# A two-layer block with Mish: the opening's loads of x and w1 cut and ordered anew

## The chip, the cores and the metric

The kernel runs on one core of one Trainium2 chip. The metric is the time of one execution on the device in microseconds, the median of several runs; lower is better. Before the change it is 105.08 us, the median of three runs from 104.75 to 105.43 us.

A core has TensorE (matrix products, from SBUF into the eight banks of PSUM), VectorE, ScalarE (activation functions), GpSimd and SyncE. In the profile they are PE (with PEld for its weight loads), DVE, ACT, POOL and SP. Loads and stores between DRAM and SBUF are DMAs. In this kernel SyncE and ScalarE issue them, each into a queue of its own, called a ring here: q1 is SyncE's and q10 ScalarE's in the profile.

## The reference

```python
B, S, D, F = 1, 2048, 512, 1792          # all bf16
h   = einsum("bsd,df->bsf", x, w1) + b1
sp  = log1p(exp(-abs(h))) + where(h > 0, h, 0)   # softplus
act = h * tanh(sp)                               # Mish
out = einsum("bsf,fd->bsd", act, w2)
```

Both products have the same number of multiplications: 2048 x 512 x 1792.

## The kernel before, in words

All sizes are cut into 128s: x has 16 tiles of 128 rows, D has 4 parts (index k), F has 14 (index f). The work goes through four blocks of 512 rows of x, that is four x tiles each (`BLOCKS`).

*First matmul* (`mm1_step`, L157, its product at L169). For each f, four products over k add up in one PSUM bank. The stationary operand is a 128x128 piece of w1, the moving one the transposed x: 128 rows (D) by up to 512 columns (rows of x). ScalarE then applies Mish with the bias (`mish`, L149) and writes the bf16 result into `a_sb`; this frees the bank.

*Second matmul* (`mm2_step`, L186). For each x tile, 14 products over f add up in a bank; `put` (L194) has VectorE copy the bank to `o_sb` and SyncE store it.

After the first block the order is regular: 14 f tiles of the first matmul, then the block's four x tiles of the second. The order of instructions on each engine is written out by hand; a wait on a semaphore stops its engine's stream, and all that comes later on that engine waits too. `wait` (L17) leaves out waits that the engine has already made.

*The opening* is where the change lies. While the first data travel, TensorE runs dummy products on a constant into bank 7 (`WARM`, L7). x is needed transposed. The first two tiles are loaded as they are into `x_nat` by one DMA on SyncE's ring (L102), a partition holding two neighbouring rows of x (2 KB in DRAM); TensorE transposes them in eight steps (`transpose_x`, L142) into banks 0 to 3, and VectorE and ScalarE in turn copy each k to `xT` (L145). The output rows of these two tiles are interleaved in the same way (`rows`, L180). All other x tiles come by DMA transpose straight into `xT`: tiles 2 and 3 at once (L103), each later block in one (L114).

w1 for the first eight f tiles comes in four DMAs, each of two k by four f tiles, with rows of 1 KB in DRAM: f 0 to 3 on ScalarE's ring, f 4 to 7 on SyncE's behind the x loads. Then SyncE loads the bias b1, the rest of w1 (768 KB), w2 (1792 KB) and the later x blocks.

In the first block, f 0 to 3 are computed on x tiles 0 and 1 (256 columns, all k), then on tiles 2 and 3 (`first`, L209). f 4 to 6 follow at 512 columns in two halves of k (`half`, L216), with the transpose of the bias (L234) between them, which reads the padded copy that VectorE makes (L230). The other f tiles follow at 512 columns.

Of the kernel before, what the change touches and what calls it, by code (L numbers as in the profile page):

```python
# [4 lines left out]

P = 128
WARM = (512,) * 5 + (256, 256)  # L7
BLOCKS = (512, 512, 512, 512)


# [21 lines left out]
def bass_standalone__dense_activation_mish__prompt_kernel(  # L32
# [20 lines left out]
    F0 = 4  # L53
    N0 = BLOCKS[0] // P

    with ExitStack() as es:
# [19 lines left out]
        sp = Stream(nc.sync, None)  # L76
# [5 lines left out]
        def load(q, dst, src, name, transpose=False):  # L82
            s = sem(name)
            (q.eng.dma_start_transpose if transpose else q.eng.dma_start)(dst, src).then_inc(s, 16)
            return (s, 16)
# [3 lines left out]

        t_w1, t_w2 = {}, {}
# [37 lines left out]

        free = [[] for _ in range(8)]
        t_cp = {(j, k): t_x23 for j in (2, 3) for k in range(KT)}
        t_mish, t_acc = {}, {}

        def transpose_x():

            pe.wait(t_xn, t_id)
            for k in range(KT):
                eng = (dve, act)[k % 2]
                psb = ps[:, k, 0:P].bitcast(BF)  # L140
                for j in range(2):
                    mm = nc.tensor.transpose(psb[:, j * P:(j + 1) * P], x_nat[:, j, k * P:(k + 1) * P], ident[:, :])  # L142
                eng.wait(pe.mark(mm))
                dst = xT[:, k, 0:2 * P]
                t = eng.mark(nc.vector.tensor_copy(dst, psb) if eng is dve else act.eng.activation(dst, psb, ACT.Copy))  # L145
                t_cp[0, k] = t_cp[1, k] = t
                free[k] = [t]

        def mish(s, f, bank, t_mm):  # L149
            n = BLOCKS[s]  # L150
            act.wait(t_b1c, t_mm)
            t = act.mark(act.eng.activation(a_sb[:, f, starts[s]:starts[s + 1]], ps[:, bank, 0:n], ACT.Mish,  # L152
                                            bias=b1_sb[:, f:f + 1]))
            t_mish[s, f] = t
            free[bank] = [t]

        def mm1_step(s, f, k, bank, js=None):  # L157

            n = BLOCKS[s]
            lo, hi = (0, n) if js is None else (js[0] * P, (js[-1] + 1) * P)  # L160
            first = k == 0 and lo == 0
            if first:
                pe.wait(*free[bank])
            pe.wait(t_w1[k, f])
            if s:
                pe.wait(t_xT[s])
            else:
                pe.wait(*[t_cp[j, k] for j in (js or range(N0))])
            return nc.tensor.matmul(ps[:, bank, lo:hi], w1_sb[:, k, f * P:(f + 1) * P],  # L169
                                    xT[:, k, starts[s] + lo:starts[s] + hi], start=first, stop=(k == KT - 1 and hi == n))  # L170
# [6 lines left out]
        s_out = sem("s_out")  # L177
        n_out = 0

        def rows(i):  # L180

            if i < 2:
                return out2[0:2 * P, :].rearrange("(p j) d -> p j d", p=P)[:, i, :]
            return out2[i * P:(i + 1) * P, :]
# [9 lines left out]
        def put(i, lo, hi, bank, t_mm):  # L194
            nonlocal n_out
            dve.wait(t_mm)
            t = dve.mark(nc.vector.tensor_copy(o_sb[:, i, lo:hi], ps[:, bank, 0:hi - lo]))  # L197
            free[bank] = [t]
            sp.wait(t)
            sp.eng.dma_start(rows(i)[:, lo:hi], o_sb[:, i, lo:hi]).then_inc(s_out, 16)  # L200
# [8 lines left out]
        def first(js, ks):  # L209
            for k in ks:  # L210
                for f in range(F0):
                    mm = mm1_step(0, f, k, 4 + f, js)
                    if k == KT - 1 and js[-1] == N0 - 1:
                        t_acc[f] = pe.mark(mm)

        def half(fs, ks):  # L216
            for f in fs:
                for k in ks:
                    mm = mm1_step(0, f, k, f - F0)
                if ks[-1] == KT - 1:  # L220
                    t_acc[f] = pe.mark(mm)
# [11 lines left out]
        psb1 = ps[:, 3, 0:P // 2].bitcast(BF)  # L233
        t_b1t = pe.mark(nc.tensor.transpose(psb1, b1_pad[:, :], ident[:, :]))  # L234
        dve.wait(t_b1t)
        t_b1c = dve.mark(nc.vector.tensor_copy(b1_sb[:, :], psb1[:, 0:FT]))  # L236
        free[3] = [t_b1c]
        for f in range(F0):
            mish(0, f, 4 + f, t_acc[f])
        half(range(F0, F0 + 3), (2, 3))  # L240
        for f in range(F0, F0 + 3):
            mish(0, f, f - F0, t_acc[f])
        for f in range(F0 + 3, FT):
            mm1(0, f, (4 + f) % 8)

        for i in range(N0):
            mm2(i, 0, D, (i + 2) % 4)
        for s in range(1, len(BLOCKS)):
            for f in range(FT):
                mm1(s, f, 4 + f % 4)  # L250
# [35 lines left out]
```

## Time and profile before

| what | value |
|---|---|
| median of three runs | 105.08 us |
| the profiled execution | 105.38 us |
| its span, first to last instruction | 104.1 us |
| TensorE busy | 100.8 us (97%) |
| ScalarE busy | 39.1 us (38%) |
| VectorE busy | 12.3 us (12%) |
| read from and written to DRAM | 3.94 and 2.10 MB |

The profile shows one execution. Times are in microseconds from the start of the span. A page of it gives each engine's busy time, the span in 40 slices, the DMA queues, the chain of work that ended last, and groups of instructions by line. Further views give the chain in order of time, the timeline of an engine, the waits, sums over stretches of time, and how long after its issue a DMA landed. Matmuls are pipelined, so that a group's busy time is not the sum of the durations of its instructions; the distance between starts is what one costs.

### The profile page before, as it was taken

To read this page: it belongs to the slowest core of one execution; us is meant where nothing else is said; L and a number is where in the kernel's file an instruction comes from. 1 tells how busy PE (TensorE), PEld (TensorE's weight loads), DVE (VectorE), ACT (ScalarE), POOL (GpSimd) and SP (SyncE) were. 2 spreads that over 40 slices of the span, in tenths; PEclk is the share of its full clock that TensorE was granted. 3 is DMA by queue.
4 is the path that set the end of the run, shared out by engine and by line. 5 is a ranking of instruction groups with operands and counts; after the bars stand their busy time and mean duration, and the time that the engine had idled before them with its cause. 6 is when DMAs were issued, how large, how long until landed. Compare 5 with 4: busy or idle time off the path is not lost.

```text
span 104.1 us, 1118 instructions
## 1 busy us (share of the span) xinstructions
PE 100.8 (97%) x485; PEld 48.2 (46%) x494; DVE 12.3 (12%) x22; ACT 39.1 (38%) x59; POOL 0.7 (1%) x6
## 2 busy tenths in 40 slices
PE   6999999999999999999999999999999999999992
PEld 2586444444444444444444444444444444444462
DVE  0200000022220000022220000022112000011223
ACT  3400999200027777200007777500005777700000
POOL 2000000000000000000000000000000000000000
PEclk9999999999999999999999999999999999999999
DMA  2999999991101000010111000001111000001111
GB/s 42 331 337 362 347 320 131 211 193 50 43 7 50 0 0 0 6 50 2 49 50 50 0 0 3 0 6 50 50 50 50 0 0 0 0 0 50 57 50 50
DMA packets 13345, 7.94 MB, mean 76 GB/s; under 512 B 7836, under 2 KB 13212, under 8 KB 13340
## 3 DMA queue, kind: packets, MB, share of 16 engines
q1 hardware_dynamic: 12796, 7.35, 27.0%
q10 hardware_dynamic: 544, 0.52, 1.4%
q8 instruction: 4, 0.07, 0.3%
q14 instruction: 1, 0.01, 0.0%
HBM read 3.94 MB, written 2.10 MB: 58 GB/s over the span
## 4 chain that ended last, share of the span: by engine, by line
PE 94%; DMA 3%; issue 1%; DVE 0%
PE ps L169 47%; PE ps L191 46%; DMA x_nat<-in_x_dram 3%; PE ps L142 1%; DVE o_sb L197 0%; PE ps L234 0%
## 5 line engine op out<-in xcount | busy, mean ns | idle before, releaser
L152 ACT ACTIVATE a_sb<-ps,b_sb 128x512 bf16<-128x512 f32 x56 | 37.1, 697 | 48.6 <-PE ps L169 43.3
L169 PE MATMUL ps<-xT,w_sb 128*128 128x512 bf16 (+1 forms) x235 | 49.3, 368 | 0.2
L191 PE MATMUL ps<-w_sb,a_sb 128*128 128x512 bf16 (+2 forms) x234 | 48.8, 366 | 0.3
L169 PEld LDWEIGHTS ps<-xT,w_sb 128*128 128x128 bf16 x240 | 23.7, 99 | 24.9
L191 PEld LDWEIGHTS ps<-w_sb,a_sb 128*128 128x128 bf16 x238 | 22.8, 98 | 25.9
L197 DVE CAST o_sb<-ps 128x512 bf16<-128x512 f32 (+2 forms) x17 | 11.2, 660 | 80.9 <-PE ps L191 80.9
L128 PE MATMUL ps<-const-bfloat16-1.0 128*128 128x512 bf16 (+1 forms) x7 | 2.7, 564 | 0.8 <-PEq L271 0.8
L122 ACT ACT_TABLE_LOAD x1 | 1.3, 1283 | 1.8 <-issue 1.8
L128 PEld LDWEIGHTS ps<-const-bfloat16-1.0 128*128 128x128 bf16 x7 | 0.9, 134 | 2.2 <-issue 2.2
L145 ACT ACTIVATE xT<-ps 128x256 bf16<-128x256 bf16 x2 | 0.8, 384 | 1.4 <-PE ps L142 1.3
L142 PE MATMUL ps<-ident,x_nat 128*128 128x128 bf16 x8 | 1.0, 311 | 0.2 <-DMA x_nat<-in_x_dram 0.2
L142 PEld LDWEIGHTS ps<-ident,x_nat 128*128 128x128 bf16 x8 | 0.8, 140 | 0.7 <-DMA x_nat<-in_x_dram 0.7
L145 DVE COPY xT<-ps 128x256 bf16<-128x256 bf16 x2 | 0.6, 292 | 3.3 <-PE ps L142 3.2
L230 DVE COPY b_pad<-b_nat 14x128 bf16<-14x128 bf16 x1 | 0.2, 183 | 3.1 <-DMA b_nat<-in_b_dram 3.1
L236 DVE CAST b_sb<-ps 128x14 f32<-128x14 bf16 x1 | 0.2, 173 | 2.2 <-PE ps L234 2.2
L120 POOL TENSOR_SCALAR_AFFINE_SELECT ident<-ones 128x128 bf16<-128x128 bf16 x1 | 0.3, 295 | 0.1
L234 PE MATMUL ps<-ident,b_pad 128*128 128x128 bf16 x1 | 0.2, 219 | 0.0
L117 DVE MEMSET b_pad<- 128x64 uint32 x1 | 0.1, 112 | 0.9 <-PEq L271 0.9
L118 POOL MEMSET ones<- 128x128 bf16 x1 | 0.2, 205 | 0.3 <-POOLq L271 0.3
L234 PEld LDWEIGHTS ps<-ident,b_pad 128*128 128x128 bf16 x1 | 0.1, 98 | 0.1
L271 POOL MEMSET const-bfloat16-1.0<- 128x1 bf16 x1 | 0.1, 102 | 0.0
L271 POOL MEMSET const-uint8-127<- 128x1 uint8 x1 | 0.1, 102 | 0.0
(2 smaller groups left out, 0.2 us busy)
## 6 DMA issues: line engine op xcount, KB each, us to landing
out_dram<-o_sb SPq DMA_DIRECT2D x15, 128.0 KB, 1.7
w_sb<-in_w_dram SPq DMA_DIRECT2D x1, 1792.0 KB, 10.4
w_sb<-in_w_dram SPq DMA_DIRECT2D x1, 768.0 KB, 5.6
w_sb<-in_w_dram ACTq DMA_DIRECT2D x2, 256.0 KB, 3.8
w_sb<-in_w_dram SPq DMA_DIRECT2D x2, 256.0 KB, 4.4
x_nat<-in_x_dram SPq DMA_DIRECT2D x1, 256.0 KB, 2.9
out_dram<-o_sb SPq DMA_DIRECT2D x1, 96.0 KB, 1.6
xT<-in_x_dram SPq DMA_TRANSPOSE x4, 5.5
```

The costliest lines, as they stand in the source:

```text
L118: t_ones = pool.mark(pool.eng.memset(ones[:, :], 1.0))
L120: t_id = pool.mark(pool.eng.affine_select(ident[:, :], ones[:, :], pattern=[[1, P]], compare_op=ALU.is_equal, fill=0.0, base=0, channel_mu ...
L122: act.eng.preload_act_table(ACT.Mish)
L128: nc.tensor.matmul(ps[:, 7, 0:n], c_w, c_m[:, 0:n], start=True, stop=True)
L142: mm = nc.tensor.transpose(psb[:, j * P:(j + 1) * P], x_nat[:, j, k * P:(k + 1) * P], ident[:, :])
L145: t = eng.mark(nc.vector.tensor_copy(dst, psb) if eng is dve else act.eng.activation(dst, psb, ACT.Copy))
L152: t = act.mark(act.eng.activation(a_sb[:, f, starts[s]:starts[s + 1]], ps[:, bank, 0:n], ACT.Mish, bias=b1_sb[:, f:f + 1]))
L169: return nc.tensor.matmul(ps[:, bank, lo:hi], w1_sb[:, k, f * P:(f + 1) * P], xT[:, k, starts[s] + lo:starts[s] + hi], start=first, stop=( ...
L191: return nc.tensor.matmul(ps[:, bank, 0:hi - lo], a_sb[:, f, i * P:(i + 1) * P], w2_sb[:, f, lo:hi], start=(f == 0), stop=(f == FT - 1))
L197: t = dve.mark(nc.vector.tensor_copy(o_sb[:, i, lo:hi], ps[:, bank, 0:hi - lo]))
L230: t_b1p = dve.mark(nc.vector.tensor_copy(b1_pad[0:FT, :], b1_nat[:, :]))
L234: t_b1t = pe.mark(nc.tensor.transpose(psb1, b1_pad[:, :], ident[:, :]))
```

## The change

- One dummy product of 256 columns is taken out.
- x tiles 0 and 1 are loaded by two DMAs of 128 KB, tile 0 on SyncE's ring, tile 1 on ScalarE's, each tile being 128 consecutive rows of x (1 KB rows). The interleaving and `rows` go.
- b1 is loaded second on ScalarE's ring.
- w1 for the first eight f tiles (`OPEN`) comes in four DMAs, each of one k and eight f tiles, with rows of 2 KB: k 0, 2 and 3 on SyncE's ring, k 1 on ScalarE's.
- The DMA transpose of x tiles 2 and 3 is issued after these.
- `transpose_x` takes one x tile at a time: two k to a bank and to a copy, VectorE k 0 and 1, ScalarE k 2 and 3.
- The first block runs k by k over eight f tiles in all eight banks (`bank0`): k 0 on tile 0 alone, then on tile 1 alone (128 columns each, f 0 to 6, as bank 7 is kept for the bias), the transpose of the bias, k 1 on both tiles, f 7 for k 0 and 1, then k 2 and 3; then tiles 2 and 3 for each f over all k, with its Mish behind it. f 8 to 13 follow at 512 columns.

```diff
-WARM = (512,) * 5 + (256, 256)
+WARM = (512,) * 5 + (256,)
...
-        for k0, k1 in ((0, 2), (2, 4)):
-            load_part(act, k0, k1, 0, F0)
-        t_xn = load(sp, x_nat[:, :, :], x2[0:2 * P, :].rearrange("(p j) d -> p j d", p=P), "s_xn")
+        for q, j in ((sp, 0), (act, 1)):
+            t_xn[j] = load(q, x_nat[:, j, :], x2[j * P:(j + 1) * P, :], "s_xn%d" % j)
+        t_b1 = load(act, b1_nat[:, :], b1.rearrange("(j p) -> j p", p=P), "s_b1")
+        for q, k in ((sp, 0), (act, 1), (sp, 2), (sp, 3)):
+            load_part(q, k, k + 1, 0, OPEN)
         t_x23 = load(sp, xT[:, :, 2 * P:4 * P], x2[2 * P:4 * P, :], "s_x23", True)
-        for k0, k1 in ((0, 2), (2, 4)):
-            load_part(sp, k0, k1, F0, 8)
-        t_b1 = load(sp, b1_nat[:, :], b1.rearrange("(j p) -> j p", p=P), "s_b1")
-        load_part(sp, 0, KT, 8, FT)
+        load_part(sp, 0, KT, OPEN, FT)
...
+        def transpose_x(j):
+            pe.wait(t_xn[j], t_id)
+            for h, eng in enumerate((dve, act)):
+                psb = ps[:, 2 * j + h, 0:P].bitcast(BF)
+                for i in range(2):
+                    k = 2 * h + i
+                    mm = nc.tensor.transpose(psb[:, i * P:(i + 1) * P], x_nat[:, j, k * P:(k + 1) * P], ident[:, :])
+                eng.wait(pe.mark(mm))
+                dst = xT[:, 2 * h:2 * h + 2, j * P:(j + 1) * P]
...
+        bank0 = (4, 5, 6, 0, 1, 2, 3, 7, 4, 5, 6, 0, 1, 2)
+
+        def first(fs, js, ks):
             for f in fs:
                 for k in ks:
-                    mm = mm1_step(0, f, k, f - F0)
...
+                    mm = mm1_step(0, f, k, bank0[f], js)
+            return mm
+
+        most, last = range(OPEN - 1), (OPEN - 1,)
         for n in WARM:
             dummy(n)
-        transpose_x()
-        first((0, 1), range(KT))
-        first((2, 3), range(KT))
-
+        transpose_x(0)
+        transpose_x(1)
+        first(most, (0,), (0,))
+        first(most, (1,), (0,))
         dve.wait(t_b1, t_bz)
         t_b1p = dve.mark(nc.vector.tensor_copy(b1_pad[0:FT, :], b1_nat[:, :]))
-        half(range(F0, F0 + 3), (0, 1))
-        pe.wait(t_b1p, *free[3])
+        pe.wait(t_b1p, *free[7])
...
+        first(most, (0, 1), (1,))
+        first(last, (0, 1), (0, 1))
+        for k in (2, 3):
+            first(range(OPEN), (0, 1), (k,))
+        for f in range(OPEN):
+            mish(0, f, bank0[f], pe.mark(first((f,), (2, 3), range(KT))))
+        for f in range(OPEN, FT):
+            mm1(0, f, bank0[f])
```

More of the change, by code (lines that the diff above doesn't have):

```diff
@@ L132, in bass_standalone__dense_activation_mish__prompt_kernel @@
         t_cp = {(j, k): t_x23 for j in (2, 3) for k in range(KT)}
[L133 to L142, printed above, removed]
-                eng.wait(pe.mark(mm))
[L144 to L147, printed above, removed]
+        t_mish = {}
+        def transpose_x(j):
[5 more added lines that the diff above has]
+                    mm = nc.tensor.transpose(psb[:, i * P:(i + 1) * P], x_nat[:, j, k * P:(k + 1) * P], ident[:, :])
+                eng.wait(pe.mark(mm))
+                dst = xT[:, 2 * h:2 * h + 2, j * P:(j + 1) * P]
+                src = psb.rearrange("p (k t) -> p k t", k=2)
+                t = eng.mark(nc.vector.tensor_copy(dst, src) if eng is dve else act.eng.activation(dst, src, ACT.Copy))
+                for i in range(2):
+                    t_cp[j, 2 * h + i] = t
+                free[2 * j + h] = [t]
         def mish(s, f, bank, t_mm):
@@ L206, in mm2 @@
             put(i, lo, hi, bank, pe.mark(mm))
[L209 to L216, printed above, removed]
+        bank0 = (4, 5, 6, 0, 1, 2, 3, 7, 4, 5, 6, 0, 1, 2)
+        def first(fs, js, ks):
             for f in fs:
                 for k in ks:
-                    mm = mm1_step(0, f, k, f - F0)
-                if ks[-1] == KT - 1:
-                    t_acc[f] = pe.mark(mm)
+                    mm = mm1_step(0, f, k, bank0[f], js)
+            return mm
+        most, last = range(OPEN - 1), (OPEN - 1,)
         for n in WARM:
             dummy(n)
-        transpose_x()
-        first((0, 1), range(KT))
-        first((2, 3), range(KT))
+        transpose_x(0)
+        transpose_x(1)
+        first(most, (0,), (0,))
+        first(most, (1,), (0,))
         dve.wait(t_b1, t_bz)
         t_b1p = dve.mark(nc.vector.tensor_copy(b1_pad[0:FT, :], b1_nat[:, :]))
-        half(range(F0, F0 + 3), (0, 1))
-        pe.wait(t_b1p, *free[3])
-        psb1 = ps[:, 3, 0:P // 2].bitcast(BF)
+        pe.wait(t_b1p, *free[7])
+        psb1 = ps[:, 7, 0:P // 2].bitcast(BF)
         t_b1t = pe.mark(nc.tensor.transpose(psb1, b1_pad[:, :], ident[:, :]))
@@ L236, in bass_standalone__dense_activation_mish__prompt_kernel @@
         t_b1c = dve.mark(nc.vector.tensor_copy(b1_sb[:, :], psb1[:, 0:FT]))
[L237 to L247, printed above, removed]
+        free[7] = [t_b1c]
+        first(most, (0, 1), (1,))
[6 more added lines that the diff above has]
+            mm1(0, f, bank0[f])
+        for i, bank in zip(range(N0), (3, 7, 0, 1)):
+            mm2(i, 0, D, bank)
         for s in range(1, len(BLOCKS)):
```

10 lines of the change are left out of this document (3 added, 7 removed).

## The prediction

> **What bounds the kernel now.** I read the page first: the busy table, then the chain that ended last; after that the chain in order of time, the timeline of each engine over the opening, and the DMA windows over the same stretch.
>
> ```profile
> PE 100.8 (97%) x485; PEld 48.2 (46%) x494; DVE 12.3 (12%) x22; ACT 39.1 (38%) x59; POOL 0.7 (1%) x6
> PEclk9999999999999999999999999999999999999999
> PE 94%; DMA 3%; issue 1%; DVE 0%
> 0.80 2.92 DMA x_nat<-in_x_dram
> 3.77 1.03 PE L142 MATMUL ps<-ident,x_nat 128*128 128x128 bf16 x8 [0.21 <-DMA x_nat<-in_x_dram]
> 17.47 12.25 PE L191 MATMUL ps<-w_sb,a_sb 128*128 128x512 bf16 x55
> ```
>
> The chain is 94% TensorE. The only other piece of size is the 2.92 us in which the first two x tiles travel (0.80 to 3.72). The transposes begin at 3.77, and from there to the end TensorE has no idle that a wait explains. The first product of the second matmul (L191) starts at 17.47; everything from there on is untouched by the diff except that two x tiles' output rows lie differently in DRAM. So the change can act only between 0.8 and 17.5 us: by when TensorE starts on real data, by how fast it runs there, and by any wait that is put in.
>
> How fast it runs can be read from the timeline, asked from successive moments: the same group is shown with fewer and fewer instructions left.
>
> ```profile
> 4.80 5.44 PE L169 MATMUL ps<-xT,w_sb 128*128 128x256 bf16 x36
> 5.66 4.58 PE L169 MATMUL ps<-xT,w_sb 128*128 128x256 bf16 x32
> 6.17 4.08 PE L169 MATMUL ps<-xT,w_sb 128*128 128x256 bf16 x29
> 8.57 1.68 PE L169 MATMUL ps<-xT,w_sb 128*128 128x256 bf16 x7
> 10.57 7.07 PE L169 MATMUL ps<-xT,w_sb 128*128 128x512 bf16 x32
> 11.65 5.99 PE L169 MATMUL ps<-xT,w_sb 128*128 128x512 bf16 x27
> L191 PE MATMUL ps<-w_sb,a_sb 128*128 128x128 bf16 x14 | 0.9, 219 | 0.0
> ```
>
> From 4.80 to 5.66 four 256-column matmuls start, one per 0.215 us. From 6.17 to 8.57 it is 22, one per 0.109. At 512 columns it is five in 1.08, or 0.216. So TensorE runs at half pace until about 6.0 us and at full pace after it, although the page's row of granted clock reads full from the first slice: that row does not show the opening, the pace does. The eight transposes take (1.03 - 0.31)/7 = 0.103 us each at the slow pace, and the last row gives about (0.9 - 0.22)/13 = 0.05 us for 128 columns at full pace, whose weight loads are therefore hidden.
>
> This sets the exchange rate of the whole case: a microsecond of real work gained **before 6.0 us is worth half a microsecond**, since there it is done at half pace.
>
> **The change part by part.** First the loads. The issues of the two rings, the data that moved, and the times to landing:
>
> ```profile
> 0.80 0.40 SPq L84 DMA_DIRECT2D x_nat<-in_x_dram  x1
> 1.26 1.30 SPq L84 DMA_TRANSPOSE xT<-in_x_dram  x1
> 2.62 1.08 SPq L84 DMA_DIRECT2D w_sb<-in_w_dram  x2
> 4.28 0.94 SPq L84 DMA_DIRECT2D w_sb<-in_w_dram  x2
> 0.79 0.99 ACTq L84 DMA_DIRECT2D w_sb<-in_w_dram  x2
> 1.60:1.80 0.20, 0.20 (x2) 0.15 (x1) 0.00 (x0) 0.00 (x0) 0.00 (x0) 1.00 0.00 0
> 1.80:2.00 0.20, 0.20 (x2) 0.00 (x0) 0.00 (x0) 0.18 (x1) 0.00 (x0) 1.00 1.40 102
> 2.00:2.20 0.20, 0.20 (x2) 0.13 (x1) 0.00 (x0) 0.20 (x1) 0.00 (x0) 1.00 1.05 61
> 2.20:2.40 0.20, 0.20 (x2) 0.02 (x1) 0.00 (x0) 0.20 (x1) 0.00 (x0) 1.00 0.43 143
> 2.40:2.60 0.20, 0.20 (x2) 0.10 (x1) 0.00 (x0) 0.20 (x1) 0.00 (x0) 1.00 0.59 225
> 2.60:2.80 0.20, 0.20 (x2) 0.04 (x1) 0.00 (x0) 0.20 (x1) 0.00 (x0) 1.00 0.96 369
> 2.80:3.00 0.20, 0.20 (x2) 0.08 (x1) 0.00 (x0) 0.20 (x1) 0.00 (x0) 1.00 1.02 374
> q1 hardware_dynamic: 88, 0.18, 73.9%
> q10 hardware_dynamic: 134, 0.14, 65.3%
> q1 hardware_dynamic: 56, 0.08, 37.2%
> DMA packets 273, 0.26 MB, mean 376 GB/s; under 512 B 16, under 2 KB 273, under 8 KB 273
> DMA packets 459, 0.12 MB, mean 235 GB/s; under 512 B 459, under 2 KB 459, under 8 KB 459
> DMA to landing us min/median/max: 5.0/5.0/5.0
> w_sb<-in_w_dram SPq DMA_DIRECT2D x1, 768.0 KB, 5.6
> ```
>
> The last number of a slice is GB/s. Nothing moves before 1.8 us. The three queue rows say: from 1.6 to 2.8 only SyncE's ring (q1) moves data; from 2.8 to 3.4 ScalarE's (q10) has 134 packets beside 56 of q1. So ScalarE's first load, issued at 0.79 like SyncE's, has its first data a microsecond later. The 376 GB/s are 1 KB rows of w1 (3.5 to 4.2), the 369 to 374 mostly 2 KB rows of x; the 235 are the DMA transpose (4.9 to 5.4); 5.0 us is the landing time of the transpose of tiles 2-3 (1.26 + 5.0 = 6.26).
>
> *x tiles 0 and 1, one per ring.* Added up, the slices give 106 KB by 2.6, 180 KB by 2.8 and 255 KB by 3.0. The 256 KB that all passed by about 3.4 on the slowest engine landed at 3.72, so I add 0.35 to a mean end. Tile 0 (128 KB) is then through at 2.66 and lands at 3.0 to 3.2, instead of 3.72 for both. Tile 1 has two ends: if ScalarE's ring starts like SyncE's, both are through at 3.0 and land at 3.35; if it starts at 2.8 to 2.9 as here, with its 65% of about 370 GB/s, 128 KB take 0.53 us and it lands at 3.75 (3.9 at half the rate). I take 3.75, the row of the same ring.
>
> *One dummy matmul less.* Five of 512 columns at 0.427 (twice 0.215) and one of 256 from 0.83 end at 3.18. Tile 0's four transposes fill 3.2 to 3.63; tile 1's run from 3.75 to 4.18.
>
> *w1 in 2 KB rows, one load per k.* The rows show no better rate for 2 KB (369) than for 1 KB (376): I take nothing. [...] k = 0 follows tile 0 on SyncE's ring: 512 KB of x and w1 are through 257/375 = 0.69 us after 3.0 and land at 4.03; if k = 1 shares the rate it is 768 KB and 4.73. I take 4.2, nearer to the first, since k = 1 is ScalarE's third issue (some 0.5 us each).
>
> *Matmuls.* The 14 of 128 columns on k = 0 run from 4.2 at 0.107 to 5.7, the bias transpose to 5.8. k = 1 must be there: 1.02 MB with k = 2 ahead of it, 5.05 + 0.35 = 5.4. One of its 256-column matmuls runs before 6.0; the other eight with k = 0 and 1 at 0.109 end at 6.9, k = 2 at 7.7, k = 3 at 8.6. k = 3 lands at 6.1 by the same count. Tiles 2-3 come as a transpose behind it: 256 KB at 235 GB/s from 5.73 is 6.85, and with as much as 0.8 us to landing 7.65, against a need at 8.6. **It moves later by 1.4 us and stays covered by 0.9 us**; if the cover is gone, each 0.1 us late costs 0.1. The rest of w1 landed at 4.28 + 5.6 = 9.9 and is needed at 8.6 + 32 x 0.109 = 12.1; SyncE has issued x, three w1 parts and the transpose by about 4.1, no later than before, so w2 and the later x keep their times.
>
> *What is queued behind the new waits.* TensorE is in order: transposes of tile 1 wait for ScalarE's ring with all of w1's work behind them. The bias transpose now stands behind the k = 0 work, with the bias issued on ScalarE at about 1.3 instead of SyncE at 3.74. ScalarE has three issues before its table load, which moves from 1.82 to about 2.3:
>
> ```profile
> 1.82 1.28 ACT L122 ACT_TABLE_LOAD   x1 [1.82 <-issue]
> L145 ACT ACTIVATE xT<-ps 128x256 bf16<-128x256 bf16 x2 | 0.8, 384 | 1.4 <-PE ps L142 1.3
> L152 ACT ACTIVATE a_sb<-ps,b_sb 128x512 bf16<-128x512 f32 x14 | 8.2, 727 | 5.3 <-DVE b_sb L236 5.3
> 15.69 3.06 ACT L152 ACTIVATE a_sb<-ps,b_sb 128x512 bf16<-128x512 f32 x5
> ```
>
> It ends at about 3.6, before the first copy is wanted (3.63 + 0.2). The second copy of tile 1 frees bank 3 for f = 6 at 4.18 + 0.2 + 0.38 = 4.8, wanted at 4.2 + 6 x 0.107 = 4.84: tight, at worst 0.2 us of slow time. The Mish activations lose their 5.3 us of wait for the bias; that is no gain, for the last of the block ended at 18.75 with its value wanted at 17.47 + 13 x 0.216 = 20.3.
>
> *More, smaller matmuls.* Sixteen of 512 columns become 14 of 128 and 25 of 256: at full pace 16 x 0.216 = 3.46 against 14 x 0.056 + 25 x 0.109 = 3.51 us, **+0.05**.
>
> **The sum.** Real work before 6.0 us: now 3.77 to 6.0, 2.23 us; after, 0.43 + 0.43 + (6.0 - 4.2) = 2.66 us. That is 0.43 us of slow time, 0.21 us of full-pace work. With +0.05 the span falls by about 0.16 us. Bounds: without any wait from 3.18 on, 0.30 - 0.05 = 0.25 faster; with k = 0 at 4.73, 0.86 + 1.27 = 2.13, so 0.05 + 0.05 = 0.1 slower. The profiled execution took 105.38 us (span 104.1 and 1.28 around it), 0.30 above the median of 105.08 and within its 104.75 to 105.43. From 105.38 the sum gives 105.22; as a median, 105.08 - 0.16 = **104.9**.
>
> **The rivals.**
>
> *The full pace comes later (slower).* Place: TensorE's wait for tile 1, or for k = 0, in the slow opening. In the kernel before, full pace came 5.2 us after the first dummy (0.83 to 6.0), across an idle of 0.21 us. If a longer idle made TensorE earn it again, counted from work at 4.2 it comes at 9.4, 3.4 us later, and half of that, 1.7 us, is lost: 106.8; less if only part of it starts anew, 106.2. It decides as soon as the idle before 6.0 is clearly above those 0.21 us; my sum has about 0.15, the late ends of tile 1 and k = 0 give 0.7. [...]
>
> *ScalarE's ring is served last.* If tile 1 waits until SyncE's k = 0, 2, 3 are through (2.66 + 768/375 = 4.7), it lands at 5.4; work before 6.0 is 0.43 + 0.6 = 1.03, a loss of 0.6 + 0.05: 105.7. Against it: 134 packets of q10 passed beside q1's.
>
> *The split brings nothing.* Both rings share the same rate (2.8 to 3.4 us shows 374 GB/s with both at work, 369 with one); if tile 0 lands with tile 1 at 3.75 to 3.9, the start is that of before and +0.05 to 0.1 remains: 105.1 to 105.5. [...]
>
> *The full pace comes earlier.* With no gap after the dummies it might come 1 us sooner: a further half microsecond, 104.4; 2 us sooner gives 103.9.
>
> **How the numbers follow.** Forecast 0.50 (104.5 to 105.2); split brings nothing 0.17; ring served last 0.08; full pace later 0.17 (106.2 to 106.8); earlier 0.08. One per cent, 1.05 us, is about what a measurement of this kernel tells from no change: faster than 104.03 is half of the last case, with 0.01 from the forecast, 0.05; slower than 106.13 is the late clock with a little of the starved ring, 0.18; the rest, 0.77, is within. A range of 104.2 to 106.4 leaves out three quarters of the late clock and half of the early one, under 0.2.
>
> **What would show it.** Right: first transposes at about 3.2, two groups of four; first w1 matmul near 4.2; full pace near 6.0; L191 starting at 17.3. Wrong: tile 1 landing after 4; a wait on tiles 2-3 before the 512-column matmuls; above all a change of pace later than 6.5, which outweighs everything else here.

## The result, and the profile after

The changed kernel takes 110.0 us (median of five runs, 108.51 to 110.11) beside 104.76 us for the kernel before (five runs, 104.5 to 105.43): a ratio of 1.0445, 95% interval 1.0367 to 1.0522. It is slower by 4.5%, where no difference was forecast. The profiled execution is one of 110.0 us. Here and below, ratios and medians leave out executions that lay more than 1.5% above the fastest one of the same kernel.

From the page of the changed kernel, first the span, the busy times, the granted clock and the chain; then the landing times of the opening's loads (the last number of each row).

```profile
span 108.7 us, 1162 instructions
PE 103.7 (95%) x507; PEld 51.5 (47%) x516; DVE 12.2 (11%) x22; ACT 39.5 (36%) x59; POOL 0.7 (1%) x6
PEclk9999999999999999999999999999999999999999
PE 88%; DMA 5%; ACT 3%; ACTq 1%; issue 1%; DVE 0%
w_sb<-in_w_dram SPq DMA_DIRECT2D x3, 256.0 KB, 5.8
w_sb<-in_w_dram ACTq DMA_DIRECT2D x1, 256.0 KB, 5.8
x_nat<-in_x_dram ACTq DMA_DIRECT2D x1, 128.0 KB, 2.8
x_nat<-in_x_dram SPq DMA_DIRECT2D x1, 128.0 KB, 2.6
```

The DMA piece of the chain is no longer x: it is a w1 part, which took 5.8 us from its issue. Before, the same amount of w1 landed in 3.8 (ScalarE's ring) and 4.4 us (SyncE's). The 3% of ScalarE in the chain are five Mish activations (14.08 to 17.09), and TensorE has no idle beside them. Next the timeline of TensorE, and two pieces of the chain in order of time:

```profile
3.47 1.03 PE L141 MATMUL ps<-ident,x_nat 128*128 128x128 bf16 x8
4.33 1.68 PE L170 MATMUL ps<-xT,w_sb 128*128 128x128 bf16 x14
5.80 0.31 PE L224 MATMUL ps<-ident,b_pad 128*128 128x128 bf16 x1
7.81 0.61 PE L170 MATMUL ps<-xT,w_sb 128*128 128x256 bf16 x2 [1.69 <-DMA w_sb<-in_w_dram]
13.81 8.40 PE L170 MATMUL ps<-xT,w_sb 128*128 128x256 bf16 x51
15.78 6.43 PE L170 MATMUL ps<-xT,w_sb 128*128 128x256 bf16 x33
22.05 2.32 PE L186 MATMUL ps<-w_sb,a_sb 128*128 128x512 bf16 x10
```

```profile
1.94 5.82 DMA w_sb<-in_w_dram
7.81 6.18 PE ps L170 x29
```

Up to 5.8 us the opening runs nearly as forecast. Then TensorE waits 1.69 us for k = 1, which ScalarE issued at 1.94 and which landed at 7.76. The chain's next piece holds 29 matmuls of 256 columns in 6.18 us, 0.213 each: that is the slow pace. From 13.81 to 15.78 it is 18 in 1.97, or 0.109. Full pace came at 13.6 us, against 6.0 before. The page's clock row again reads full throughout, but in the trace the records of the granted clock begin only at 13.63 us (6.01 before), and the row counts a time without a record as full. The second matmul starts at 22.05 instead of 17.47, 4.58 us later, and the span is 4.6 longer: all of the loss lies here.

It can be summed in the prediction's own way. Real work at the slow pace: before 2.23 us (3.77 to 6.0), now 2.65 (3.47 to 6.12) and 5.82 (7.81 to 13.63), 8.47 in all. The difference of 6.24 us costs half, 3.12. With 1.69 of waiting, 0.05 for the smaller matmuls and 0.30 off for the earlier start this is 4.56. So **about two thirds of the loss is pace and one third is the wait itself.** What the DMA engines moved in that stretch (last column GB/s; the one before it their busy share, which goes over 1 because a packet is counted whole in the stretch where it starts):

```profile
3.50:4.00 0.50, 0.50 (x6) 0.50 (x7) 0.10 (x1) 0.11 (x1) 0.00 (x0) 1.00 1.12 209
4.00:5.00 1.00, 1.00 (x12) 0.82 (x11) 0.57 (x3) 0.77 (x2) 0.00 (x0) 1.00 0.86 252
5.00:6.00 1.00, 1.00 (x11) 0.85 (x9) 0.00 (x0) 0.00 (x0) 0.00 (x0) 1.00 0.98 309
6.00:7.00 1.00, 0.12 (x2) 0.00 (x0) 0.17 (x1) 0.00 (x0) 0.00 (x0) 1.00 2.03 230
7.00:8.00 1.00, 0.19 (x2) 0.13 (x3) 0.00 (x0) 0.00 (x0) 0.00 (x0) 1.00 0.32 60
```

The prediction let them move 375 GB/s here. They were about fully busy up to 6 us (0.86 to 1.12), and yet slow: in the trace's packet records, 2 KB packets of w1, which take 0.084 us in the median, took 0.2 to 1.1 us in 26 cases between 3.5 and 5.8 us. After that a few pieces are late: 13 of the 16 increments of k = 1 had come by 6.47, the last three at 6.99, 7.58 and 7.76; from 7 to 8 us only 60 GB/s move. The four w1 parts were complete at 4.25 (k = 0), 7.76 (k = 1), 7.56 (k = 2) and 8.34 (k = 3).

### The profile page after: what moved, and what is told of

It reads as the page before. It is cut to its first block, busy times and chain, and to the rows that moved or that the text cites. A ratio compares the mean times of both kernels' runs of the same rounds, so it can differ in the third digit from the quotient of the medians.

```text
span 108.7 us, 1162 instructions
## 1 busy us (share of the span) xinstructions
PE 103.7 (95%) x507; PEld 51.5 (47%) x516; DVE 12.2 (11%) x22; ACT 39.5 (36%) x59; POOL 0.7 (1%) x6
## 2 busy tenths in 40 slices
DMA packets 12977, 7.94 MB, mean 73 GB/s; under 512 B 7852, under 2 KB 12460, under 8 KB 12972
## 4 chain that ended last, share of the span: by engine, by line
PE 88%; DMA 5%; ACT 3%; ACTq 1%; issue 1%; DVE 0%
PE ps L186 44%; PE ps L170 44%; DMA w_sb<-in_w_dram 5%; ACT a_sb L153 3%; ACTq L84 1%; DVE o_sb L192 0%; ACTq L24 0%
## 5 line engine op out<-in xcount | busy, mean ns | idle before, releaser
L170 PE MATMUL ps<-xT,w_sb 128*128 128x512 bf16 (+2 forms) x259 | 52.6, 367 | 1.9 <-DMA w_sb<-in_w_dram 1.7
L170 PEld LDWEIGHTS ps<-xT,w_sb 128*128 128x128 bf16 x263 | 27.1, 106 | 26.6 <-DMA w_sb<-in_w_dram 2.0
```

## The experiments

Landings below are the last of a load's increments of its semaphore in the profile of that run; "the wait" is TensorE's.

**e1: k = 1 on SyncE's ring too.**

```diff
-        for q, k in ((sp, 0), (act, 1), (sp, 2), (sp, 3)):
+        for q, k in ((sp, 0), (sp, 1), (sp, 2), (sp, 3)):
```

> All four w1 parts of the first eight f tiles go on SyncE's ring, in the order k 0, 1, 2, 3; ScalarE's ring keeps x tile 1 and the bias. Theory A (k = 1 and k = 2 in 2 KB rows on two rings at once hinder each other): the parts come one after the other at 340 to 375 GB/s, k = 1 lands at about 4.9 to 5.3 instead of 7.76, TensorE does not wait for it, full pace comes at 5 to 7 us and the time is 104.5 to 105.5. Theory B (the DMA transpose queued behind w1 disturbs the loads before it) or C (2 KB rows of w1 at their distance of 3584 B are slow after the first part): the stretch from 3.5 to 8 us stays at 50 to 320 GB/s, the last w1 part lands at about 8.3 as in the changed kernel, and the time stays above 107.

Measured: 106.26 us, ratio to before 1.0128 (1.0091 to 1.0165). k = 1 landed at 6.21 and the wait shrank to 0.08 us, full pace came at about 7.1; but k = 2 and 3 landed only at 6.83 and 8.01, with packets of up to 1.45 us. So w1 on two rings at once is not needed for the stalls. With the parts in the order of their use the same slow stream hurts much less. Some of what is left lies elsewhere: w2 landed at 18.64 (15.09 in the kernel before), and TensorE waited 0.58 us for it ahead of the second matmul.

**e2: the transpose of tiles 2-3 behind all of w1.**

```diff
-        t_x23 = load(sp, xT[:, :, 2 * P:4 * P], x2[2 * P:4 * P, :], "s_x23", True)
         load_part(sp, 0, KT, OPEN, FT)
+        t_x23 = load(sp, xT[:, :, 2 * P:4 * P], x2[2 * P:4 * P, :], "s_x23", True)
```

> The DMA transpose of x tiles 2 and 3 is issued after the rest of w1 (768 KB) instead of ahead of it. Theory B (the queued transpose disturbs): k = 1 lands before 5.6 and the wait for it (1.7 us in the changed kernel) goes; a wait of about 2.5 us for tiles 2 and 3 comes at 8.6 instead. Theories A and C: k = 1 still lands after 7 and k = 2 too; the wait for it stays at 1.2 us or more. The time is 107 to 111 by all, so the landing of k = 1 tells them apart.

Measured: 108.14 us (one run). k = 1 at 7.98, k = 2 at 7.79, and k = 0 itself late, at 5.65, with a wait of 1.31 us (the wait for k = 1 is then 0.56). The queued transpose is not what disturbs.

**e3: the same parts in 1 KB rows.**

```diff
-            load_part(q, k, k + 1, 0, OPEN)
+            for a in (0, 4):
+                load_part(q, k, k + 1, a, a + 4)
```

> Each w1 part is loaded by two DMAs of four f tiles each, with 1 KB rows, on the same rings in the same order. Theory C (2 KB rows are the cause): k = 1 lands by about 5.6 to 6 and the wait for it is under 0.3 us. Theory A (two rings at once, whatever the rows) and B: k = 1 lands after 7, the wait stays over 1 us and the time over 108.

Measured: 106.38 us (one run). The halves of k = 1 landed at 5.76 and 6.90, the last w1 part at 7.89, with stalls from 3.6 to 5 us; TensorE waited 0.25 and 0.58 us for k = 0, and full pace came early, by 4.7; 0.33 us more went on a wait for w2. Between the two expectations: a little sooner, not cured.

**e4: TensorE kept at work through the wait.**

```diff
+        for n in (256,) * 9:
+            dummy(n)
         pe.wait(t_b1p, *free[7])
```

> The changed kernel with nine dummy products of 256 columns (1.92 us at the slow pace) ahead of the bias transpose, so that TensorE works through the wait for k = 1. If the late full pace is due to that idle: full pace comes between 5 and 7.7 us instead of 13.6, TensorE then waits a little for k = 3 and tiles 2-3, the second matmul starts at about 19.2 instead of 22.05, and the time is about 107 (106.5 to 107.8). If the pace depends on something else: no change from 110, or slower by the dummies.

Measured: 107.55 us, ratio to before 1.0268 (1.0237 to 1.03), 2.45 us less than the changed kernel's 110.0. The timeline of TensorE:

```profile
5.15 1.67 PE L170 MATMUL ps<-xT,w_sb 128*128 128x128 bf16 x14 [0.83 <-DMA w_sb<-in_w_dram]
6.62 2.08 PE L127 MATMUL ps<-const-bfloat16-1.0 128*128 128x256 bf16 x9
8.54 0.22 PE L226 MATMUL ps<-ident,b_pad 128*128 128x128 bf16 x1
8.59 1.15 PE L170 MATMUL ps<-xT,w_sb 128*128 128x256 bf16 x9
9.79 10.37 PE L170 MATMUL ps<-xT,w_sb 128*128 128x256 bf16 x70
20.00 0.81 PE L186 MATMUL ps<-w_sb,a_sb 128*128 128x512 bf16 x3
```

The loads were as late as before the edit (k = 1 at 8.02; k = 0 this time at 5.11, hence the 0.83), but by 8.5 the pace is full: nine matmuls take 1.15 us. Nothing but useless work was added. That the idle here costs pace, and that filling it gives back about half of the loss, is shown.

**e5: w1 in the old blocks of two k by four f tiles.**

```diff
-        for q, k in ((sp, 0), (act, 1), (sp, 2), (sp, 3)):
-            load_part(q, k, k + 1, 0, OPEN)
+        for q, k, a in ((sp, 0, 0), (act, 0, 4), (sp, 2, 0), (sp, 2, 4)):
+            load_part(q, k, k + 2, a, a + 4)
```

> The changed kernel, rings and order of issues kept, but w1's first eight f tiles in the blocks of the kernel before: two k by four f tiles, 1 KB rows (k 0-1 of f 0 to 3 on SyncE's ring, of f 4 to 7 on ScalarE's, then k 2-3 of both on SyncE's). Theory E (a load of one k alone is what the DMA engines stall on, as it was in all four kernels so far): no packets of 0.4 us and more between 3.5 and 6 us, k 0-1 landed by 5, full pace at 5 to 7, time 104.3 to 105.3. Theory F (what stalls is early w1 traffic as such, with x and the bias ahead of it on two rings): the stalls stay and the time is 106 or more.

Measured: 106.65 us (one run). The profile is of an execution of 111.3 us, so only its loads are read: the block on ScalarE's ring landed at 8.41 and TensorE waited 3.44 us for it, after stalls of up to 0.87 us from 3.48 on. One k per load is not the cause.

**e6 and e13: the bias on SyncE's ring, behind k = 3.** One kernel, run twice.

```diff
-        t_b1 = load(act, b1_nat[:, :], b1.rearrange("(j p) -> j p", p=P), "s_b1")
...
+        t_b1 = load(sp, b1_nat[:, :], b1.rearrange("(j p) -> j p", p=P), "s_b1")
         t_x23 = load(sp, xT[:, :, 2 * P:4 * P], x2[2 * P:4 * P, :], "s_x23", True)
```

> The changed kernel with the bias load moved from ScalarE's ring to SyncE's, behind k = 3. Theory D (the small bias load, 14 pieces of 256 B on 14 of the 16 engines, upsets the engines' order): the stalls from 3.5 us go, k = 1 lands by 5.6, time 104.5 to 106. Theory E or F: k = 1 still lands after 6.5 and the time is 107 to 110.5.

> The same kernel as the one with the bias moved to SyncE's ring behind k = 3, a second time. If its stall-free loads belong to that order of issues: again no packet of 0.5 us and more from 3.5 us on, x tiles 2-3 landed by 7.9, times within 0.5 of 107.7. If that was chance: stalls from 3.5 us and times up to 110.

Measured: 107.69 us (one run), and 106.38 and 107.37 (ratio 1.0179, 1.0127 to 1.023). Landing times of the second run, and its timeline of TensorE; its profile is of an execution of 109.25 us:

```profile
w_sb<-in_w_dram SPq DMA_DIRECT2D x3, 256.0 KB, 4.5
w_sb<-in_w_dram ACTq DMA_DIRECT2D x1, 256.0 KB, 3.6
```

```profile
3.75 1.04 PE L141 MATMUL ps<-ident,x_nat 128*128 128x128 bf16 x8 [0.40 <-DMA x_nat<-in_x_dram]
5.05 1.67 PE L170 MATMUL ps<-xT,w_sb 128*128 128x128 bf16 x14 [0.26 <-DMA w_sb<-in_w_dram]
7.45 0.29 PE L224 MATMUL ps<-ident,b_pad 128*128 128x128 bf16 x1 [0.73 <-DVE b_pad L221]
```

The loads agree in both runs: k = 1 at 4.73 and 4.81 (7.76 with the bias ahead of it), k = 2 at 5.76 and 6.26, k = 3 at 6.73 and 6.93 (8.34), tiles 2-3 at 7.75 and 7.98 (9.40). Stalls in w1 are few and short, 0.28 us at most in the first run and 0.45 in the second. So the place of the bias load makes w1 late, though not by its own size: the load is 3.5 KB. (With the bias load gone from ahead of it k = 1 is also issued sooner, at 1.22 instead of 1.94; that could be 0.7 of the 3 us.) The times did not follow, for a plain reason that I had missed in the expectation: the bias now lands at 7.0 to 7.2, its transpose stands ahead of k = 1 in TensorE's order, and TensorE idles for it (0.57 and 0.73 us); full pace then came at 9.3 in the first run. The second run's packets met its expectation; tiles 2-3 (7.98 for 7.9) and the times did not.

**e7: the kernel before, with w1 one k per load, in 2 KB rows.**

```diff
-        for k0, k1 in ((0, 2), (2, 4)):
-            load_part(act, k0, k1, 0, F0)
+        for k in (0, 1):
+            load_part(act, k, k + 1, 0, 8)
...
-        for k0, k1 in ((0, 2), (2, 4)):
-            load_part(sp, k0, k1, F0, 8)
+        for k in (2, 3):
+            load_part(sp, k, k + 1, 0, 8)
```

> The kernel before, with one edit: w1's first eight f tiles in four loads of one k each with 2 KB rows (k 0 and 1 on ScalarE's ring, 2 and 3 on SyncE's), at the places of its four loads. Theory E: stalls of 0.4 us and more appear, the last w1 part lands some 1 us later than 7.7 and the time is 106 or more. Theory D or F: no stalls, time 104.4 to 105.6.

Measured: 106.25 us (one run), and no stalls in these four loads (0.27 us at most); the last part at 7.42, a little sooner than 7.7. The time is lost elsewhere: x landed at 4.31 instead of 3.72, and k = 2, now needed by f 0 to 3, is waited for at 6.8. By the loads, this again speaks against theory E.

**e8: bias late, its transpose after k = 3, and all of w1 on SyncE's ring.**

```diff
-WARM = (512,) * 5 + (256,)
+WARM = (512,) * 5 + (256, 256)
...
-        t_b1 = load(act, b1_nat[:, :], b1.rearrange("(j p) -> j p", p=P), "s_b1")
-        for q, k in ((sp, 0), (act, 1), (sp, 2), (sp, 3)):
+        for q, k in ((sp, 0), (sp, 1), (sp, 2), (sp, 3)):
             load_part(q, k, k + 1, 0, OPEN)
+        t_b1 = load(sp, b1_nat[:, :], b1.rearrange("(j p) -> j p", p=P), "s_b1")
...
+        for k in range(1, KT):
+            first(most, (0, 1), (k,))
...
-        first(most, (0, 1), (1,))
-        first(last, (0, 1), (0, 1))
-        for k in (2, 3):
-            first(range(OPEN), (0, 1), (k,))
+        first(last, (0, 1), range(KT))
```

> The changed kernel with the bias load last of the small loads on SyncE's ring, its transpose after the k = 3 pass over f 0 to 6 (f 7 follows it), all w1 parts on SyncE's ring, and the dummy product put back that the change took out. If the bias on ScalarE's ring and the idle that follows from it are the whole cause, this is the opening as the prediction saw it: x tiles at about 3.5, k = 0 at about 4.2, parts 0.7 us apart, no wait after 4.5, full pace at 5 to 7, time 104.5 to 105.2, the same as the kernel before or up to 0.3 faster. If something else in the change costs time too, 105.8 or more.

Measured: 106.2 us, ratio 1.0096 (1.0062 to 1.0129). From TensorE's timeline, the group that begins with k = 1:

```profile
6.44 2.47 PE L170 MATMUL ps<-xT,w_sb 128*128 128x256 bf16 x21 [0.72 <-DMA w_sb<-in_w_dram]
```

The expectation fails in the loads: with no bias load ahead of w1, packets stalled from 3.49 to 4.6 us (up to 1.0 us), k = 1 came at 6.40 and was waited for 0.72 us. The bias is therefore not the only thing that makes early w1 loads stall. The pace did as expected: it was full from 5.1 us, and 21 matmuls in 2.47 us right behind the wait show that it stayed so. The wait cost its own length and no pace.

**e9: the kernel before, with the bias second on ScalarE's ring.**

```diff
-        for k0, k1 in ((0, 2), (2, 4)):
-            load_part(act, k0, k1, 0, F0)
+        load_part(act, 0, 2, 0, F0)
+        t_b1 = load(act, b1_nat[:, :], b1.rearrange("(j p) -> j p", p=P), "s_b1")
+        load_part(act, 2, 4, 0, F0)
...
-        t_b1 = load(sp, b1_nat[:, :], b1.rearrange("(j p) -> j p", p=P), "s_b1")
```

> The kernel before, with one edit: the bias load stands second on ScalarE's ring, between its two w1 loads. If the bias load there is the cause by itself: stalls of 0.4 us and more in w1's and x's packets from about 3.5 us, later w1 landings, a wait in the opening, and 106 or more. If it does harm only beside the changed loads: 104.4 to 105.4, no stalls.

Measured: 106.12 us, ratio 1.0097 (1.0061 to 1.0134). Its windows, then its timeline of TensorE:

```profile
3.40:4.40 1.00, 0.83 (x8) 0.68 (x8) 0.24 (x1) 0.36 (x2) 0.00 (x0) 1.00 1.22 299
4.40:5.40 1.00, 1.00 (x9) 0.73 (x7) 0.43 (x3) 0.74 (x2) 0.00 (x0) 1.00 1.23 192
5.40:6.40 1.00, 0.51 (x5) 0.20 (x3) 0.00 (x0) 0.00 (x0) 0.00 (x0) 1.00 1.06 200
```

```profile
4.60 1.31 PE L169 MATMUL ps<-xT,w_sb 128*128 128x256 bf16 x8
7.37 1.81 PE L169 MATMUL ps<-xT,w_sb 128*128 128x256 bf16 x15 [1.47 <-DMA w_sb<-in_w_dram]
```

In the same three stretches the kernel before moved these:

```profile
3.40:4.40 1.00, 0.79 (x8) 0.64 (x8) 0.20 (x1) 0.00 (x0) 0.00 (x0) 1.00 1.06 371
4.40:5.40 1.00, 1.00 (x8) 0.72 (x7) 0.38 (x2) 0.77 (x2) 0.00 (x0) 1.00 1.25 256
5.40:6.40 1.00, 1.00 (x9) 0.76 (x7) 0.00 (x0) 0.00 (x0) 0.00 (x0) 1.00 1.13 314
```

One small load put between two large ones on ScalarE's ring took 64 to 114 GB/s off the stream, let the load behind it land at 7.33 instead of 5.30, and cost a wait of 1.47 us. The step does harm by itself. The pace was full from 5.2 us and is full directly behind this wait too (15 matmuls in 1.81 us). Here no packet stalled for longer than about 0.3 us, so the form is not quite that of the changed kernel.

**e10: the bias second on SyncE's ring.**

```diff
-        t_b1 = load(act, b1_nat[:, :], b1.rearrange("(j p) -> j p", p=P), "s_b1")
+        t_b1 = load(sp, b1_nat[:, :], b1.rearrange("(j p) -> j p", p=P), "s_b1")
```

> The changed kernel with the bias load second on SyncE's ring, behind x tile 0, instead of second on ScalarE's. If what matters is that the bias load is early (ahead of w1), on whichever ring: stalls from 3.5 us, k = 1 after 6.5, 107 to 110.5. If what matters is ScalarE's ring: no stalls, k = 1 by 5.6, 104.5 to 106.

Measured: 107.72 us (one run). k = 1, now alone behind x on ScalarE's ring, landed at 4.21; k = 0, behind the bias, at 5.78, with a wait of 1.09 us; stalls from 3.56 to 5.4 us. Neither branch fits whole, since k = 1 came early and the time is over 106. So it is not ScalarE's ring as such: what stands behind the early bias load comes late.

**e11: the bias as 16 rows.**

```diff
-        b1_nat = sb("b1_nat", [FT, P], BF)
+        b1_nat = sb("b1_nat", [16, 112], BF)
...
-        t_b1 = load(act, b1_nat[:, :], b1.rearrange("(j p) -> j p", p=P), "s_b1")
+        t_b1 = load(act, b1_nat[0:16, 0:112], b1.rearrange("(j p) -> j p", p=112), "s_b1")
...
-        t_b1p = dve.mark(nc.vector.tensor_copy(b1_pad[0:FT, :], b1_nat[:, :]))
+        t_b1p = dve.mark(nc.vector.tensor_copy(b1_pad[0:16, 0:112], b1_nat[:, :]))
```

> The changed kernel with the bias loaded at the same place as 16 rows of 224 B instead of 14 rows of 256 B, so that it can be spread evenly over 16 DMA engines. The bias values then reach the wrong rows: the right bias is left out, the work is the same. If the uneven spread over 14 engines is the cause: the bias semaphore is raised 16 times, no stalls, k = 1 by 5.6, 104.5 to 106. If a small load there is enough: stalls as in the changed kernel and 107 to 110.5.

Measured: 108.31 us (one run); the semaphore was raised 16 times, k = 1 landed at 7.57, the wait was 1.59 us. So the bias coming in 14 pieces instead of 16 is not the cause.

**e12: the transpose of tiles 2-3 second on SyncE's ring.**

```diff
+        t_x23 = load(sp, xT[:, :, 2 * P:4 * P], x2[2 * P:4 * P, :], "s_x23", True)
         t_b1 = load(act, b1_nat[:, :], b1.rearrange("(j p) -> j p", p=P), "s_b1")
...
-        t_x23 = load(sp, xT[:, :, 2 * P:4 * P], x2[2 * P:4 * P, :], "s_x23", True)
```

> The changed kernel with the DMA transpose of x tiles 2 and 3 back at its old place, second on SyncE's ring ahead of w1. Theory H (a w1 load that has its turn on the engines within about 1.8 us of its issue stalls; behind the transpose it has its turn later): SyncE's k = 0, 2 and 3 flow without stalls of 0.4 us from 4.5 us on, but k = 0 lands only at 5.3 or later, so that TensorE waits for it and the time stays at 106 to 108.5. Theory J (stalls come with early w1 traffic wherever it stands): stalls remain and 107 to 110.

Measured: 109.46 and 109.83 us, ratio 1.0443 (1.0401 to 1.0485). Tile 1 landed at 4.83, the transposed tiles at 7.46 (6.24 in the kernel before, from the same place) and k = 0 at 7.94, with a wait of 2.50 us for it. With the bias on ScalarE's ring the old place of the transpose is no better. Theory H is left open: behind the transpose SyncE's three parts did flow (7.94, 8.60 and 9.27, with one packet of 0.52 us), while 15 packets of ScalarE's k = 1 took 0.4 to 0.6 us; but k = 0 came at 7.94 where H had 5.3 or a little later, and the time is theory J's.

**e14: w1's rows taken from where rows have no gaps.**

```diff
-            return load(q, w1_sb[:, ks, a * P:b * P], w1v[:, ks, a * P:b * P], "s_w1_%d_%d" % (ks.start, a))
+            src = w1v[:, ks, a * P:b * P]
+            if a == 0:
+                k = ks.start
+                src = w2.rearrange("(r two) d -> r (two d)", two=2)[k * P:(k + 1) * P, :].unsqueeze(1)
+            return load(q, w1_sb[:, ks, a * P:b * P], src, "s_w1_%d_%d" % (ks.start, a))
```

> The changed kernel, but the four loads of w1's first eight f tiles read 2 KB rows that lie one behind the other (rows of w2) instead of w1's rows 3584 B apart; the values of these w1 tiles are thereby left out, the work is the same. If the stalls come from how w1's rows lie in DRAM: no stalls, k = 1 by 5.6, 104.5 to 106. If they come from the queues: stalls from 3.5 us as in the changed kernel, 107 to 110.5.

Measured: 108.83 us (one run), stalls from 3.5 to 5.5 us, k = 1 at 7.77. So the gaps between w1's rows in DRAM are not the cause.

**e15: k = 0 and 1 first, on ScalarE's ring; x tiles 0 and 1 on SyncE's.** Otherwise as e8; the diff is against e8.

```diff
-        for q, j in ((sp, 0), (act, 1)):
+        load_part(act, 0, 1, 0, OPEN)
+        for q, j in ((sp, 0), (sp, 1)):
             t_xn[j] = load(q, x_nat[:, j, :], x2[j * P:(j + 1) * P, :], "s_xn%d" % j)
-        for q, k in ((sp, 0), (sp, 1), (sp, 2), (sp, 3)):
+        for q, k in ((act, 1), (sp, 2), (sp, 3)):
             load_part(q, k, k + 1, 0, OPEN)
```

> k = 0 and k = 1 are issued first and second on ScalarE's ring, x tiles 0 and 1 first and second on SyncE's, then k = 2, k = 3 and the bias on SyncE's; the bias transpose after the k = 3 pass and the dummy product put back as in the late-bias kernel. Theory H: every w1 load has 2 us or more between issue and turn, no stalls, the parts land by 4.5, 4.7, 5.6 and 6.4, time 104.5 to 105.4. Theory J: stalls and 106 or more.

Measured: 106.35 us, ratio 1.0128 (1.0095 to 1.0161). The parts landed at 3.83, 4.97, 6.31 and 6.99, the first sooner than expected and the last two 0.6 to 0.7 us later, with few stalls but one of 0.75 us: not what theory H says. Tile 1 of x came at 5.13, and TensorE idled 0.52 and 0.71 us for the two tiles, at full pace from its first transposes on.

**e16: the change without its bias step.** As e8, but with k = 1 on ScalarE's ring; the diff is against e8.

```diff
-        for q, k in ((sp, 0), (sp, 1), (sp, 2), (sp, 3)):
+        for q, k in ((sp, 0), (act, 1), (sp, 2), (sp, 3)):
```

> The changed kernel with the bias on SyncE's ring behind k = 3 and its transpose after the k = 3 pass, so that it waits for nothing; k = 1 stays on ScalarE's ring; the dummy product put back. If the bias on ScalarE's ring is what made the change slow, w1's parts land by 5.0, 5.0, 6.3 and 7.0 as in the two runs with the bias moved, TensorE idles about 0.1 and 0.3 us before k = 0 and not after, full pace comes at 5.5 to 8, the second matmul starts at 17.7 to 18.5 and the time is 105.0 to 105.9: no gain over the kernel before, since x and k = 0 come no sooner than there. If more of the change is at fault: 106.2 or more.

Measured: 106.03 us, ratio 1.0062 (1.0031 to 1.0093). The timeline of TensorE:

```profile
3.71 1.04 PE L141 MATMUL ps<-ident,x_nat 128*128 128x128 bf16 x8 [0.15 <-DMA x_nat<-in_x_dram]
5.02 4.08 PE L170 MATMUL ps<-xT,w_sb 128*128 128x128 bf16 x35 [0.27 <-DMA w_sb<-in_w_dram]
9.42 9.28 PE L170 MATMUL ps<-xT,w_sb 128*128 128x256 bf16 x60 [0.27 <-DVE b_sb L228]
18.54 0.81 PE L186 MATMUL ps<-w_sb,a_sb 128*128 128x512 bf16 x3
```

The waits for w1 after k = 0 are gone, and of the 5.2 us of loss 0.7 is left (106.03 beside 105.34 for the kernel before, measured with it); full pace came at 6.8. This is the expected cause, but the time lies between the two branches. The order of loads is that of e6, and so are the landings of k = 1 (4.71) and, less closely, of k = 2 and 3 (6.57 and 7.24); two packets stalled for 1.0 and 1.3 us this time, so how long single packets stall differs from run to run. What is left above the kernel before: work on w1 starts at 5.02 where it started at 4.64, since x and k = 0 come no sooner with k = 1 beside them, and 0.27 us is this variant's own (f 7 waits for the bias copy that reads its bank).

**e17: as e16, with 384 columns of dummy products ahead of k = 0.**

```diff
         transpose_x(1)
+        for n in (256, 128):
+            dummy(n)
```

> As the kernel without the bias step, with two more dummy products (384 columns, 0.32 us at the slow pace) between the transposes and k = 0. If the pace follows from unbroken work, full pace comes no later than 7 and the time is 104.9 to 105.5 with less spread between runs; if the idle of 0.3 us does not matter, the same as without them within 0.3.

Measured: 106.27 us (106.21 to 106.58), ratio 1.0102 (1.0057 to 1.0146). Full pace at 6.5, and the four times lie within 0.4 us, but the time is not better than e16's: the second branch. No version that was run beats the kernel before.

## Why the prediction was wrong

*Right:* k = 0 was put at 4.2 and landed at 4.25; work on it started at 4.33; the bias transpose, due from 5.7 to 5.8, started at 5.80. The tiles came at 3.4 and 3.6 for a forecast of 3.0 to 3.2 and 3.75, so that the eight transposes ran in one group; ScalarE's ring moved its first packets at 1.96 us, where the prediction took 2.8 to 2.9. The smaller matmuls cost the forecast 0.05 us within the sum above. The exchange rate of one half for work at the slow pace holds too: with it the sum above meets the measured 4.58 within 0.02. That work on k = 0 began on time although tile 0 was 0.2 to 0.4 us late is in part luck: tile 1 came sooner than was taken, and the forecast break between the tiles fell away.

*The step that failed* is the sentence on k = 1: "1.02 MB with k = 2 ahead of it, 5.05 + 0.35 = 5.4". It carried a rate of 375 GB/s, read from the kernel before between 2.6 and 4.2 us, over to a stretch whose queue was made up otherwise; the runs showed 209 to 309 GB/s up to 6 us and 60 after 7, and k = 1 at 7.76. The same false rate made k = 3 land at 8.34 for 6.1 and tiles 2-3 at 9.40 for 7.65. The bias load was counted as nothing but an issue of some 0.5 us (it took 0.68). Moving it away (e6, e13) brought k = 3 to 6.7 to 6.9 and tiles 2-3 to 7.75 to 7.98, near the forecast of 6.1 and 7.65. Putting it into the kernel before alone (e9) cost 1%.

*The right rival was there, and undersized.* "The full pace comes later" is what happened, but three things were off. The idle was placed at tile 1 and k = 0, while the wait came at k = 1. Its rule (any idle clearly above 0.21 us) does not hold: before k = 0 TensorE idled 0.8 us in e7 and 0.52 and 0.71 us in e15, and had full pace by 5.2 us in both, sooner than the kernel before (6.0). And its price was set at a pace that returns 3.4 us late, where it returned 7.6 us late (13.6 for 6.0): 106.8 instead of 110. The recorded changes of the clock in e14 and e5 lie 3.41 us or twice that apart; counted back from 13.63 in steps of that length, an estimate, the wait of 1.69 us lay across the edge between two of them, and full pace came after neither (last section).

*Not settled:* why packets of early w1 loads stall. The place of the bias load is shown to matter (e6 and e13 against the changed kernel, e9 against the kernel before), but e8 stalls without it. In the changed kernel, e1 to e5, e11 and e14, with the bias second on ScalarE's ring, the last w1 part of the opening landed at 7.9 to 8.6 (9.3 in e12, with the transpose ahead of it); in e6, e8, e13 and e15 to e17, with it behind w1, at 6.7 to 7.8. Whether the small load itself does this, or the later issue of what stands behind it, is not separated: e8, with k = 1 issued at 1.75 and no early bias load, lands k = 1 and 3 at 6.40 and 7.76, much as e1 does with one (6.21 and 8.01). Two rings, 2 KB rows, one k per load, the bias's 14 pieces, the gaps between w1's rows in DRAM and the queued transpose are each not needed for the stalls, most of them by one profile each. Free of long stalls are the profiles of before and e7; those of e6 and e13 nearly are, while e16 and e17, with the loads of e6 in the same order, again had some of 0.8 to 1.3 us. In all of these no bias load stands ahead of a w1 load, and ScalarE's ring has a w1 load as its first or second. Why this should help was not found.

## What to carry to other kernels

The DMA rate read from the queue order of before (375 GB/s) did not hold for that of the changed kernel (209 to 309 up to 6 us). Before such a rate is used for another order, the forecast needs the case in which the stream slows, priced through to the engine that waits. In the changed kernel's opening, at TensorE's slow pace until 13.6 us, the wait of 1.69 us cost its own length and, by the sum above, 3.12 us more through the late full pace, the larger part; once the pace was full, waits of 0.72 us (e8) and 1.47 us (e9) cost their own length alone. And a tiny load among large ones (3.5 KB among 256 KB, 1% by itself in e9) is an edit of its own, to be tried by itself.

## What the runs showed of the hardware that was not expected

With a 3.5 KB load second on ScalarE's ring, the 256 KB load behind it landed 2 us later in e9 (7.33 for 5.30) and about 3 later in the changed kernel (7.76 against 4.73 and 4.81), of which the later issue could be 0.7.

Packets of a DMA transpose were open for far longer than usual: in the packet records of the changed kernel, 16 packets of 256 B start between 6.40 and 7.58 us, behind w1, and all end at 8.18 to 8.21, where the median packet of 256 B takes 0.018. In the kernel before, 22 of them start between 16.80 and 17.67 us and all end at 18.57 to 18.61, while a fetch of instructions (16 KB, from 16.33 us) takes 1.89 us. What holds them was not shown.

The moment of full pace did not follow the length of the idle alone: with an idle of 0.8 us in e7 it came sooner than with 0.21 us in the kernel before. It first came at 3.7 to 5.2 us in e15, e5, e7, e3, e14, e8 and e9, at 6.0 before, at 6.5 to 7.0 in e17, e16 and e1, at 8.5 to 9.3 in e4, e2, e6 and e10, at 10.4 to 12.4 in e11, e12 and e13, and at 13.6 in the changed kernel. The records of the granted clock show a part of it. In e14 the granted clock rose at 4.80 us, fell and rose again; here are the stretches between its recorded changes (behind the comma TensorE's busy time; third from the end the granted clock):

```profile
4.80:8.22 3.42, 1.28 (x17) 0.96 (x15) 0.17 (x1) 0.15 (x1) 0.00 (x0) 1.00 1.06 254
8.22:11.63 3.41, 3.41 (x18) 2.37 (x17) 0.00 (x0) 0.00 (x0) 0.00 (x0) 0.50 1.08 349
11.63:15.04 3.41, 3.41 (x33) 3.04 (x32) 0.00 (x0) 2.11 (x4) 0.00 (x0) 1.00 1.10 347
```

After the stretch that was busy for 1.28 of 3.42 us (37%) the granted clock was 0.50, after the one busy throughout it was 1.00 again. In e5 the recorded changes lie at 4.10, 7.51 and 14.34 us, 3.41 and 6.83 apart. So in these two profiles all recorded changes lie 3.41 us or twice that apart. If the same steps are counted back from the first record of the changed kernel, at 13.63 us (an estimate: it has no earlier record), its stretches were these (the clock of 1.00 in them stands for no record; the pace was slow until 13.6):

```profile
3.39:6.80 3.41, 2.65 (x23) 2.21 (x23) 0.84 (x4) 0.99 (x3) 0.00 (x0) 1.00 1.24 269
6.80:10.22 3.42, 2.41 (x12) 1.74 (x13) 0.00 (x0) 0.00 (x0) 0.00 (x0) 1.00 0.88 217
10.22:13.63 3.41, 3.41 (x18) 2.43 (x17) 0.00 (x0) 0.00 (x0) 0.00 (x0) 1.00 1.09 356
```

By this count the one wait of 1.69 us (6.12 to 7.81) left two stretches busy for 78% and 71%, and the pace stayed slow after both; it became full after the third, busy throughout. The kernel before was busy for 94% of the 3.41 us from 2.60 to its first record at 6.01, and had full pace from there. That the clock goes by how busy TensorE was in the step that ends is an estimate from these stretches of three profiles (e14, before and the changed kernel), in which a matmul's end is modelled; what share brings the full pace, and what share keeps it, was not shown. Once full, the pace stayed through the waits of 0.72 us (e8) and 1.47 us (e9). The first recorded change lay at 4.10 us in e5, 4.80 in e14, 6.01 before and 13.63 in the changed kernel; if the estimate holds, what a wait costs depends on where in such a step it falls.
